# Seven block products in place of eight in the second feed-forward product of an attention and feed-forward kernel

## The chip, the cores and the metric

The kernel runs on one core of a Trainium2 chip, as one launch. The metric is the device time of that launch in microseconds; lower is better.

## The reference

Cosine attention over 8 batches of 12 heads, 448 positions of 64 values, and then a feed-forward block with a hard-swish over all 3584 tokens:

```python
q_n = q / (np.linalg.norm(q, axis=-1, keepdims=True) + 1e-06)
k_n = k / (np.linalg.norm(k, axis=-1, keepdims=True) + 1e-06)
scores = np.matmul(q_n, k_n.transpose(0, 1, 3, 2)) / tau
scores = scores - np.max(scores, axis=-1, keepdims=True)
attn = np.exp(scores)
attn = attn / (np.sum(attn, axis=-1, keepdims=True) + 1e-09)
x = np.matmul(attn, v)            # to (8 * 448, 12 * 64)
h = x @ w_in                      # 768 x 2048
relu6 = np.clip(h + 3.0, 0.0, 6.0)
g = h * relu6 / 6.0
return (g @ w_out)                # 2048 x 768, fp32
```

## The kernel before

**Tiling.** An *item* `i` is a pair of heads of one batch; a batch `b` has six, so there are 48 items. For an item, `scores` (L394) makes seven matmuls in four groups: the groups 0 to 2 have two matmuls each, with 64 rows of the array apiece, the fourth has one. `exps` (L412, ScalarE) turns them into `at`, `values` (L433) multiplies by `v` into the PSUM tile `PV`, `finish_values` (L453 and L454, VectorE) divides by the row sums, and a transposing DMA (`back_crossbar`, `back_two`) puts the result into `xT`, the input of the feed-forward block for this batch.

Around this, GpSimd squares the raw q and k (`square`, L203), normalises them (`normalise`, L246) and casts v (`vcast`, L265); VectorE sums the squares (`reduce`, L215); ScalarE makes the inverse norms (`norms`, L231 to L234). SP issues the loads (`load_qk`, `load_v`), the transposes and the stores. Raw items lie in 7 buffers, values in 3, squares in 2.

The feed-forward block is cut into *units*. `mm1_unit(b, fc)` is one of 16 slices of `x @ w_in` of a batch: six matmuls of 448 columns (L513) into one PSUM bank, then `relu` on ScalarE (L522) and `product` on VectorE (L528), which reads the bank too and writes the slice of g, in bf16, to `gT`. Only `product` frees the bank. `mm2_unit(b, t, m)` is one token tile of 128 and one half of 384 output columns of `g @ w_out`: 16 matmuls (L549), then a copy out of PSUM (L560 on ScalarE and L562 on VectorE by turns) and two stores.

**Order.** Every engine works through its own instructions in the order in which the program issues them; waits between engines are put in by data. The program's order is written by hand: up to item 17 in the strings of `PLAN`, from then on in a loop over items (L699 to L742). An iteration issues on TensorE: the score groups 0 to 2 of item `i`, the rest of the values of item `i - 1`, the fourth score group of `i`, then this iteration's units, and at last the first group of values of `i`.

**Banks.** After the start the PSUM has a ring of six banks, which `scores` and all units take by turns (`next_bank`). The groups 0 to 2 of an item take six, so each bank of the ring, the sixth being that of the unit issued just before.

**Where the units go.** `units[i]` holds the units of iteration `i`. Six iterations, `n` = 0 to 5, make a *turn*: in the turn of batch `b`, the `mm1_unit`s of batch `b - 1` and the `mm2_unit`s of `b - 2` are spread over them. Each list ends with the `mm2_unit`s:

```python
units[(b + 1) * HP + n] = carry + lag[: n_lag[n]] + u if n == 0 else carry + u + lag[: n_lag[n]]
```

(here `u` are `mm1_unit`s, and for n = 0 from the third batch on `u` is empty). What is left after item 47 runs in the tail: the rest of batch 6, then batch 7. The last unit of all is split into two halves of 192 columns.

`gT` has two tiles, each for two batches, 896 columns. An odd batch has four token tiles and an even one three, since the 64 tokens that an even batch leaves over are joined with 64 of the next.

Of the kernel before, what the change touches and what calls it, by code (L numbers as in the profile page):

```python
# [61 lines left out]
def kernel(  # L62
# [39 lines left out]
    gT = [const.tile([128, FCN, 2 * S], BF16, name=f"gT{i}", tag=f"gT{i}") for i in range(2)]  # L102
# [11 lines left out]
    NV, NR = 3, 7  # L114
    vr = [const.tile([128, 4, 5, D], FP32, name=f"vr{i}", tag=f"vr{i}") for i in range(NV)]
    NVX = 4
    vx = [const.tile([128, 8, D + 1], BF16, name=f"vx{i}", tag=f"vx{i}") for i in range(NVX)]
    raws = [const.tile([128, 2, 7, D], FP32, name=f"raw{i}", tag=f"raw{i}") for i in range(NR)]
    sqs = [const.tile([128, 2, 7, D], FP32, name=f"sq{i}", tag=f"sq{i}") for i in range(2)]
# [46 lines left out]
    def load_qk(j, *heads):  # L166
        needs(("NM", j - NR))
        raw_of[j] = raws[j % NR]
# [9 lines left out]
    def load_v(d):  # L178
        needs(("VC", 2 * (d - NV)), ("VC", 2 * (d - NV) + 1))
        b, n = 2 * d // HP, 2 * d % HP  # L180
        for g in range(2):
            f = v[b, HP * g + n : HP * g + n + 2].rearrange("i (p c) d -> p i (c d)", c=7)
            t = vr[d % NV][:, 2 * g : 2 * g + 2, :, :].rearrange("p i c d -> p i (c d)")
            for half in range(2):
                o = t[64 * half : 64 * half + 64, :, (1 - half) * D : (5 - half) * D]
                nc.sync.dma_start(out=o, in_=f[:, :, 3 * half * D : (3 * half + 4) * D])

    def square(j, e, c0, n):

        heads = range(c0 // 7, (c0 + n - 1) // 7 + 1) if j < 2 else (0, 1)  # L190
        needs(("RE", j - 2), *(("LQ", j, g) for g in heads))
        if j not in sq_of:
            sq_of[j] = sqs[j % 2], []
# [63 lines left out]
    def vcast(i, e):  # L257
        needs(("LV", i // 2), ("VA", i - NVX, 3))
        t = vr[i // 2 % NV][:, i % 2, 1:5, :]
# [247 lines left out]
    def mm1_unit(b, fc):  # L507
        needs(*(("CX", i) for i in range(b * HP, (b + 1) * HP)))
        assert len(weights) <= 6 - 2 * (2 * fc // FCN)
        x, g, c0 = xT[b % 2], gT[(b // 2) % 2], (b % 2) * S  # L510
# [29 lines left out]
    def mm2_unit(b, t, m, end=None):  # L540
        assert not weights
        g = gT[(b // 2) % 2]
        ps, key = bank_of(None, 1)
        width = MH if end is None else MH // 2
        cols = slice(m * MH + width * (end or 0), m * MH + width * (end or 0) + width)
        for fc in range(FCN):
            c0 = (S + SR) * (b % 2) + 128 * t if t < 3 else SM
            lhs = g[:, fc, c0 : c0 + 128]
            nc.tensor.matmul(  # L549
                ps[:, 0:width],  # L550
                lhs,
# [3 lines left out]
            )  # L555

        def store():
            o = sb.tile([128, MH], FP32, name="o", tag="o", bufs=4)
            if on_act:
                nc.scalar.copy(out=o[:, 0:width], in_=ps[:, 0:width])  # L560
            else:
                nc.vector.tensor_copy(out=o[:, 0:width], in_=ps[:, 0:width])  # L562
            unread[key] = 0
            for e in range(2):
                if t < 3:
                    r = out[b * S : (b + 1) * S].rearrange("(p c) m -> c p m", c=7)[2 * t + e + b % 2]
                else:
                    r = out[(b - 1 + e) * S : (b + e) * S].rearrange("(p c) m -> c p m", c=7)[6 * (1 - e)]
                eng = nc.scalar if end == 1 and e else nc.sync
                eng.dma_start(out=r[:, cols], in_=o[64 * e : 64 * e + 64, 0:width])  # L570

        evac_n[0] += 1
        on_act = evac_n[0] % 2 == 1
        post["a" if on_act else "v"].append(store)

    def second(b):
        nt = 3 + b % 2
        u = [(mm2_unit, b, t, m) for t in range(nt) for m in range(2)]
        return u if b < B - 1 else u[:-1] + [u[-1] + (0,), u[-1] + (1,)]

    units = {}
    carry, lag = [], []
    for b in range(B - 1):
        first = [(mm1_unit, b, fc) for fc in range(FCN)]
        n_lag = [0, 0, 1, 1, 2, 2] if b == 1 else [1, 1, 1, 1, len(lag) // 2 - 2, len(lag) // 2 - 2]
        n_first = [1, 3, 3, 3, 2, 2] if carry else [3, 3, 2, 2, 2, 2]
        if b > 1:
            n_first = [0, 3, 3, 3, 3, 2]  # L590
# [194 lines left out]
```

## Time and profile before

| | us |
|---|---|
| median of 3 runs | 423.14 |
| lowest, highest | 422.41, 423.39 |
| profiled execution: its span, from the first to the last instruction | 420.0 |

The profiled execution stands for itself: its span leaves out what lies before the first and after the last instruction, and is 3.1 us under the median of the runs. The granted clock was 0.999.

Some groups of the page that the change touches:

| line, engine | what | count | mean ns of one |
|---|---|---|---|
| L513 TensorE | `mm1_unit`, 448 columns, into M, Y and Z | 768 | 353 |
| L549 TensorE | `mm2_unit`, 384 columns | 880 | 326 |
| L549 TensorE | `mm2_unit`, 192 columns | 32 | 246 |
| L522 ScalarE | relu out of PSUM | 128 | 650 |
| L528 VectorE | product out of PSUM to bf16 | 128 | 620 |
| L560 ScalarE | copy of 384 out of PSUM | 28 | 478 |
| L562 VectorE | copy of 384 out of PSUM | 27 | 558 |
| L203 GpSimd | squares of 896 | 36 | 1679 |
| L246 GpSimd | normalise 896 | 44 | 1686 |
| L265 GpSimd | cast of 512 | 44 | 631 |

How to read it: a matmul's time runs from its issue to its modelled end; the next is issued long before that, so the time that TensorE needs for one is the distance between starts (0.19 us for 448 columns). In the timeline a row is one or several instructions on an engine: start, length, engine, line, operation, tiles, shape, count, and in square brackets how long the engine had been idle and what ended that. In the table by stretches each engine has its busy time and, in brackets, its instructions.

### The profile page before, as it was taken

Reading aid. Unit: us, or ns where it says so; the run is one execution under the profiler, and the core shown is the slowest. Engines: PE = TensorE matmul, PEld = TensorE weight load, DVE = VectorE, ACT = ScalarE, POOL = GpSimd, SP = SyncE. Lnnn points to the kernel's source line nnn. Section 1 sums busy time; section 2 is a strip of 40 time slices with the busy share of each in tenths; the row PEclk is TensorE's granted clock in tenths of the full one; section 3 lists DMA queues with packets and bytes.
Section 4 is the critical chain, followed back from the end, with each engine's and each line's share of the span. In section 5 each row is a group of like instructions: output and inputs, shape, how many; then the busy total and the mean of one; then the engine's idle time right before and its main releaser. Section 6 shows DMA issues by size and latency. Waiting matters only on the chain.

```text
span 420.0 us, 9243 instructions
## 1 busy us (share of the span) xinstructions
PE 412.6 (98%) x3600; PEld 244.6 (58%) x3600; DVE 217.3 (52%) x419; ACT 271.0 (65%) x591; POOL 183.6 (44%) x190
## 2 busy tenths in 40 slices
PE   7999999999999999999999999999999999999996
PEld 5666556556665565555565555555555555655554
DVE  6898677855345654455536454465454443315410
ACT  6899988887558666757747765866765774105400
POOL 7899646444237347257356355365462200000000
PEclk9999999999999999999999999999999999999999
DMA  8999999789796965966885858756953441330033
GB/s 296 311 235 248 182 270 229 154 152 242 202 181 133 190 162 132 179 166 140 190 196 118 191 146 171 186 157 135 193 158 72 85 66 34 70 75 21 0 77 75
DMA packets 91563, 65.29 MB, mean 155 GB/s; under 512 B 56064, under 2 KB 89984, under 8 KB 91520
## 3 DMA queue, kind: packets, MB, share of 16 engines
q1 hardware_dynamic: 87728, 58.37, 59.8%
q0 software_dynamic: 3712, 6.29, 8.6%
q8 instruction: 28, 0.46, 0.5%
q14 instruction: 15, 0.12, 0.1%
q10 hardware_dynamic: 80, 0.05, 0.0%
HBM read 47.19 MB, written 11.01 MB: 139 GB/s over the span
## 4 chain that ended last, share of the span: by engine, by line
PE 96%; DVE 1%; POOL 1%; DMA 1%; ACT 0%; issue 0%; ACTq 0%; DVEq 0%
PE M L513 24%; PE M L549 23%; PE PV L433 12%; PE Z L549 7%; PE M L394 6%; PE Y L513 6%; PE Y L549 6%; PE Z L513 5%; PE Y L394 2%; PE Z L394 1%; PE PV L620 1%; PE SC L394 1%; POOL nrm L246 1%; DMA raw<-in_k_dram 1%; PE Z L291 1%; DVE n L215 0%
## 5 line engine op out<-in xcount | busy, mean ns | idle before, releaser
L549 PEld LDWEIGHTS <-gT 128*128 128x128 bf16 x912 | 88.6, 98 | 58.4
L412 ACT ACTIVATE at<-M 128x448 bf16<-128x448 f32 x199 | 96.8, 567 | 31.2 <-PE M L394 18.9
L513 PEld LDWEIGHTS <-w_in_sb 128*128 128x128 bf16 x768 | 73.7, 98 | 65.8 <-issue 2.7
L513 PE MATMUL M<-xT,w_in_sb 128*128 128x448 bf16 x522 | 107.3, 353 | 0.0
L549 PE MATMUL M<-w_out_sb,gT 128*128 128x384 bf16 (+1 forms) x592 | 99.3, 324 | 0.0
L246 POOL TENSOR_TENSOR nrm<-raw,r 128x896 bf16<-128x896 f32 (+1 forms) x48 | 77.7, 1624 | 43.8 <-ACT r L234 34.7
L528 DVE SCALAR_TENSOR_TENSOR gT<-u,M 128x448 bf16<-128x448 bf16 x87 | 54.0, 620 | 52.3 <-ACT u L522 50.8
L203 POOL TENSOR_TENSOR sq<-raw 128x896 f32<-128x896 f32 (+3 forms) x39 | 63.4, 1627 | 9.9 <-DMA raw<-in_k_dram 4.8
L433 PEld LDWEIGHTS <-at 128*128 128x128 bf16 x1344 | 53.5, 98 | 24.4 <-issue 16.8
L522 ACT ACTIVATE u<-M,bias 128x448 bf16<-128x448 f32 x87 | 56.5, 650 | 16.6 <-PE M L513 15.4
L433 PE MATMUL PV<-vx,at 128*128 128x65 bf16 (+1 forms) x1344 | 64.0, 198 | 0.3 <-DVE on L454 0.2
L215 DVE TENSOR_REDUCE n<-sq 128x14 f32<-128x896 f32 (+1 forms) x50 | 51.8, 1041 | 3.8 <-ACT sq L201 3.6
L351 POOL COPY km<-tT 64x128 bf16<-64x128 bf16 x34 | 9.8, 289 | 96.8 <-DMA tT<-nrm 46.4
L412 ACT ACTIVATE at<-Z 128x448 bf16<-128x448 f32 x48 | 27.1, 565 | 12.5 <-PE M L394 12.4
L560 ACT COPY o<-M 128x384 f32<-128x384 f32 (+1 forms) x19 | 8.9, 470 | 40.5 <-PE M L549 40.4
L562 DVE COPY o<-M 128x384 f32<-128x384 f32 x18 | 10.0, 558 | 47.0 <-PE M L549 32.6
L454 DVE TENSOR_TENSOR on<-PV,rc 128x512 bf16<-128x512 f32 x48 | 33.2, 691 | 1.7
L394 PE MATMUL M<-tT,kz 64*128 64x448 bf16 (+1 forms) x175 | 32.6, 353 | 0.0
L549 PE MATMUL Z<-w_out_sb,gT 128*128 128x384 bf16 (+1 forms) x176 | 29.1, 319 | 0.0
L265 POOL CAST vx<-vr 128x512 bf16<-128x512 f32 x44 | 27.6, 631 | 1.5 <-DMA vr<-in_v_dram 1.5
L453 DVE RECIPROCAL rc<-PV 128x8 f32<-128x8 f32 x48 | 9.9, 207 | 34.9 <-PE PV L433 34.2
L412 ACT ACTIVATE at<-Y 128x448 bf16<-128x448 f32 x47 | 26.7, 569 | 1.7 <-PE Z L394 1.5
(78 smaller groups left out, 352.6 us busy)
## 6 DMA issues: line engine op xcount, KB each, us to landing
vr<-in_v_dram SPq DMA_DIRECT2D x96, 128.0 KB, 4.2
raw<-in_k_dram SPq DMA_DIRECT2D x24, 448.0 KB, 4.4
raw<-in_q_dram SPq DMA_DIRECT2D x24, 448.0 KB, 4.3
out_dram<-o SPq DMA_DIRECT2D x110, 96.0 KB, 2.2
w_in_sb<-in_moe_w_in_dram POOLq DMA_DIRECT2D x4, 768.0 KB, 12.2
w_out_sb<-in_moe_w_out_dram POOLq DMA_DIRECT2D x4, 768.0 KB, 9.2
tT<-nrm SPq DMA_TRANSPOSE x34, 3.3
xT<-on SPq DMA_TRANSPOSE x25, 3.9
```

Source lines behind the costliest of these rows:

```text
L203: engines[e].tensor_tensor(out=o, in0=i, in1=i, op=ALU.mult)
L215: nc.vector.tensor_reduce(out=n2s[d % 2][:, j % 2, c], in_=sq[:, :, :, :].rearrange("p g c d -> p (g c) d")[:, c, :], axis=AX.X, op=ALU.add,)
L246: engines[e].tensor_tensor(out=nrm[:, :, g, :].rearrange("p c g d -> p g c d"), in0=raw_of[j][:, g, :, :], in1=rs[d % 2][3][:, j % 2, :] . ...
L265: (engines[e].copy if e == "a" else engines[e].tensor_copy)(out=o, in_=f)
L394: nc.tensor.matmul(o, ks, qt[rows], start=True, stop=True)
L412: nc.scalar.activation(out=o, in_=x, func=AF.Exp, scale=inv_tau)
L433: nc.tensor.matmul(o, at[:, n, q_cols(i // HP, j)], mv, start=(name == "A0" and j % 2 == 0), stop=last, skip_group_check=True,)
L454: nc.vector.tensor_tensor(out=on[:, :, :, :].rearrange("p (b j) h d -> p b (j h) d", b=2), in0=pv4[:, :, :, 0:D], in1=rc[:, :, :].to_broad ...
L513: nc.tensor.matmul(ps[:, 0:S], w_in_sb[:, cc, fc * 128 : (fc + 1) * 128], x[:, cc, 0:S], start=(cc == 0), stop=(cc == CC - 1),)
L522: nc.scalar.activation(out=u[:, :], in_=ps[:, 0:S], func=AF.Relu, bias=half_bias, scale=1.0 / 6.0)
L528: nc.vector.scalar_tensor_tensor(out=g[:, fc, c0 : c0 + S], in0=u[:, :], scalar=1.0, in1=ps[:, 0:S], op0=ALU.min, op1=ALU.mult,)
L549: nc.tensor.matmul(ps[:, 0:width], lhs, w_out_sb[:, fc, cols], start=(fc == 0), stop=(fc == FCN - 1),)
```

## The change

**The products.** Two token tiles and the two halves of the output columns, with g and `w_out` split into even and odd slices `fc`, are four block products of two terms each: eight products of eight matmuls. From batch 2 on these are replaced by Strassen's seven: with A for g and B for `w_out`, sums of blocks of A and of B are formed first, seven products "1" to "7" of eight matmuls are made, and their sums are the four results. `product_unit` makes one of them. "2" is added in PSUM on top of "4" in the same bank, "5" on top of "3" and "6" on top of "1", after the first of each has been read: "4" is copied by ScalarE to `d`, "3" is added to it by VectorE, "2" and "5" are copied out and stored, GpSimd makes two differences from them, and VectorE adds those to "1", "6" and "7". An odd batch is two pairs of tiles. An even batch is one pair and a single tile, which `single_unit` makes in the old number of products but in four units of 192 columns.

**The sums.** `weight_sums` makes the sums of `w_out`, on VectorE, in the turn of batch 3: three into the new tile `w_sum`, and two (`y3`, `y4`) in place in `w_out_sb`, each once the old units of batch 1 have read that half. `g_sums` makes those of g, on VectorE, in bf16, twice for each batch, after the slices fc = 7 and fc = 15: five operations, some in place, and a sixth for the single tile. `g_left` copies the 64 columns that an even batch leaves over.

**The layout.** `gT` is one tile for even and one for odd batches. `w_sum` takes the place of two raw buffers, one value buffer and one square buffer, which are used until it is written; from then on there are 5, 2 and 1.

**The order.** The units of an iteration are put together by `turn`. The iterations up to item 17 and their `PLAN` are as they were.

```diff
+    def raw_before(j):
+        return j - 7 if j < 26 else j - 5
...
+    def value_buffer(d):
+        return vr[d % 3 if d < 12 else 1 + d % 2]
+    def square_buffer(j):
+        return sqs[j % 2 if j < 20 else 0]
...
-        x, g, c0 = xT[b % 2], gT[(b // 2) % 2], (b % 2) * S
+        x, g, c0 = xT[b % 2], gT[b % 2], (b % 2) * SR
...
+    def weight_sums(what, c0, n):
+        w = w_out_sb[:, :, :].rearrange("p (c k) m -> p c k m", k=2)[:, c0 : c0 + n]
+        b11, b12, b21, b22 = (w[:, :, k, m] for k in range(2) for m in (LEFT, RIGHT))
...
+        o, x, y, op = {
+            "x1": (w_sum[:, 0, c0 : c0 + n, :], b11, b22, ALU.add),
+            "x2": (w_sum[:, 1, c0 : c0 + n, :], b11, b12, ALU.add),
+            "x3": (w_sum[:, 2, c0 : c0 + n, :], b21, b22, ALU.add),
+            "y3": (b12, b12, b22, ALU.subtract),
+            "y4": (b21, b21, b11, ALU.subtract),
+        }[what]
+        nc.vector.tensor_tensor(out=o, in0=x, in1=y, op=op)
...
+    def g_sums(b, half):
+        c = slice(half * KC // 2, (half + 1) * KC // 2)
+        n = 1 + b % 2
...
+        todo = [
+            (s6, a21, a11, ALU.subtract),
+            (a21, a21, a22, ALU.add),
+            (s7, a12, a22, ALU.subtract),
+            (a12, a12, a11, ALU.add),
+            (s1, a11, a22, ALU.add),
+        ]
+        if n == 1:
+            e = gT[0][:, :, 256:384].rearrange("p (c k) n -> p c k n", k=2)[:, c]
+            todo.append((gs[0][:, 3, c, :], e[:, :, 0, :], e[:, :, 1, :], ALU.add))
+        for o, x, y, op in todo:
+            nc.vector.tensor_tensor(out=o, in0=x, in1=y, op=op)
...
+    def product_unit(b, g, name, end=None):
...
+        base = {"2": "4", "5": "3", "6": "1"}.get(name)
+        if base is None:
+            banks[n + (name,)] = bank_of(None, 1)
+        ps, key = banks.pop(n + (base,)) if base else banks[n + (name,)]
+        c0, width = (0, MH) if end is None else (MH // 2 * end, MH // 2)
+        for c in range(KC):
+            nc.tensor.matmul(
+                ps[:, 0:width],
+                quarter(b, g, name, c),
+                w_quarter(name, c)[:, c0 : c0 + width],
+                start=(base is None and c == 0),
+                stop=(c == KC - 1),
...
+        def copied(t, cols, x):
+            o = out_tile()
+            nc.scalar.copy(out=o[:, :], in_=m)
+            parts[n, x] = o
+            done(t, o, cols)
+        def added(t, cols, x, c0=0):
+            o = out_tile()
+            nc.vector.tensor_tensor(out=o[:, 0:width], in0=m, in1=x[:, c0 : c0 + width], op=ALU.add)
+            done(t, o, slice(cols.start + c0, cols.start + c0 + width))
+        def finish():
+            if name == "4":
+                nc.scalar.copy(out=part("d"), in_=m)
+            elif name == "3":
+                d = parts[n, "d"][:, :]
+                nc.vector.tensor_tensor(out=d, in0=m, in1=d, op=ALU.add)
+            elif name == "2":
+                copied(t2, LEFT, "C21")
+            elif name == "5":
+                copied(t1, RIGHT, "C12")
+                d = parts[n, "d"][:, :]
+                nc.gpsimd.tensor_tensor(out=part("f"), in0=d, in1=parts[n, "C12"][:, :], op=ALU.subtract)
+                nc.gpsimd.tensor_tensor(out=d, in0=d, in1=parts[n, "C21"][:, :], op=ALU.subtract)
+            elif name == "1":
+                f = parts[n, "f"][:, :]
+                nc.vector.tensor_tensor(out=f, in0=m, in1=f, op=ALU.add)
+            elif name == "6":
+                added(t2, RIGHT, parts[n, "d"])
+            else:
+                added(t1, LEFT, parts[n, "f"], c0)
...
+    def firsts(b, *fcs):
+        u = []
+        for fc in fcs:
+            u.append((mm1_unit, b, fc))
+            if b > 1 and fc % KC == KC - 1:
+                u.append((g_sums, b, fc // KC))
+        return u
...
+    def turn(b, n):
+        fc = 3 * (n - 1)
+        f = firsts(b - 1, *range(fc, fc + 3 + (n == 5))) if n else []
+        if b % 2 == 0:
+            p = [
+                products(b - 2, 0, "4325"),
+                products(b - 2, 0, "16"),
+                products(b - 2, 0, "7"),
+                singles(b - 2, (0, 0), (0, 1)),
+                singles(b - 2, (1, 0)),
+                singles(b - 2, (1, 1)),
+            ][n]
+        else:
+            p = [
+                products(b - 2, 0, "4325"),
+                products(b - 2, 0, "16"),
+                products(b - 2, 0, "7") + products(b - 2, 1, "42"),
+                products(b - 2, 1, "35"),
+                products(b - 2, 1, "16"),
+                products(b - 2, 1, "7"),
+            ][n]
+        if n == 0:
+            return p if b % 2 else [(g_left,)] + p
+        if len(p) < 3:
+            return p[:1] + f[:2] + p[1:] + f[2:]
+        return mixed([p[1], p[0], p[2]], f)
...
+    for n in range(HP):
+        fc = 3 * (n - 1)
+        if n == 0:
+            u = [(g_left,)] + firsts(1, FCN - 2, FCN - 1) + [late.pop(0) for _ in range(3)]
+        else:
+            f = firsts(2, *range(fc, fc + 3 + (n == 5)))
+            u = [late.pop(0)] + f
+        x = [(weight_sums, w, c, 2) for w in ("x1", "x2", "x3") for c in range(0, KC, 2)][3 * n : 3 * n + 3]
+        if n == 4:
+            x = [(weight_sums, "y4", c, 2) for c in range(0, KC, 2)]
+        if n == 5:
+            x = [(weight_sums, "y3", c, 2) for c in range(0, KC, 2)]
+        units[3 * HP + n] = u[:1] + x + u[1:] if n else u[:-1] + x + u[-1:]
...
+    last += products(b, 0, "4325176") + products(b, 1, "43251")
+    last += [(product_unit, b, 1, "7", 0)] + products(b, 1, "6") + [(product_unit, b, 1, "7", 1)]
```

`mixed` takes units from its two lists by turns. In the loop, sums and `g_left` are issued just before the unit that follows them in the list; they are not counted as units.

## The prediction

> **What bounds the kernel now.** I read first the page's busy time and the chain that ended last:
>
> ```profile
> PE 412.6 (98%) x3600; PEld 244.6 (58%) x3600; DVE 217.3 (52%) x419; ACT 271.0 (65%) x591; POOL 183.6 (44%) x190
> ...
> PE 96%; DVE 1%; POOL 1%; DMA 1%; ACT 0%; issue 0%; ACTq 0%; DVEq 0%
> PE M L513 24%; PE M L549 23%; PE PV L433 12%; PE Z L549 7%; PE M L394 6%; PE Y L513 6%; PE Y L549 6%; PE Z L513 5%; PE Y L394 2%; PE Z L394 1%; PE PV L620 1%; PE SC L394 1%; POOL nrm L246 1%; DMA raw<-in_k_dram 1%; PE Z L291 1%; DVE n L215 0%
> ```
>
> TensorE is the chain, so a matmul taken away is time gained, unless something new stops TensorE. The table by stretches says that it has no slack, and that VectorE, where the change puts its additions, is half idle:
>
> ```profile
> 200.00:250.00 50.00, 50.00 (x430) 29.25 (x429) 25.79 (x45) 33.95 (x77) 25.41 (x25) 1.00 0.71 166
> ```
>
> (columns: PE, PEld, DVE, ACT, POOL.) The chain in order of time gives the prices on TensorE: a unit of `mm1_unit` 1.14 us, 16 matmuls of 384 columns 2.60 us, so 0.1625 us each. The last unit's halves of 192 columns took 1.32 and 1.33 us for 16:
>
> ```profile
> 286.62 1.14 PE M L513 x6
> 287.76 1.13 PE Y L513 x6
> 288.89 1.14 PE Z L513 x6
> 290.02 2.60 PE M L549 x16
> 292.63 0.24 PE PV L433 x8
> ```
>
> Then I looked at the place where one attention item hands over to the next, because the change alters what stands in front of it. The timeline of TensorE, and VectorE beside it:
>
> ```profile
> 252.21 0.41 PE L433 MATMUL PV<-vx,at 128*128 128x65 bf16 x8
> 252.55 0.55 PE L394 MATMUL M<-tT,kz 64*128 64x448 bf16 x3
> 252.75 0.35 PE L394 MATMUL Y<-tT,kz 64*128 64x448 bf16 x1
> 252.94 0.35 PE L394 MATMUL Z<-tT,kz 64*128 64x448 bf16 x1
> 253.03 0.35 PE L394 MATMUL M<-tT,kz 64*128 64x448 bf16 x1
> 253.31 0.89 PE L433 MATMUL PV<-vx,at 128*128 128x65 bf16 x20
> ```
> ```profile
> 252.41 0.56 DVE L562 COPY o<-M 128x384 f32<-128x384 f32 x1 [1.31 <-PE M L549]
> ```
>
> The six score matmuls take all six banks of the ring, so the sixth needs the bank of the unit issued last. Here that is an `mm2_unit`; VectorE had copied it out at 252.97, and the sixth score matmul began 0.06 us later, 0.09 after its partner. Where ScalarE makes the copy (268.77 plus 0.48) it comes in time. So the kernel as it is loses about 0.05 us at each hand-over, and the reader sees how tight the place is.
>
> **The change, part by part.**
>
> *Matmuls.* Batches 2 to 7 have nine pairs of token tiles (one in each even batch, two in each odd one). A pair took 64 matmuls and takes 56: 9 x 8 x 0.1625 = 11.7 us less. The single tile of batches 2, 4 and 6 keeps its work but in four units of 192 columns: 4 x 1.325 against 2 x 2.60, 0.1 us more each, 0.3. **Gain 11.4 us**.
>
> *The order at the hand-over.* Before, a stretch of units ended with `lag`, an `mm2_unit`. In `turn` it ends with `f[2:]` (or the last of `mixed`), an `mm1_unit`, whose bank is free only after ScalarE's relu and then VectorE's product. What that takes is in the rows of the last 16 `mm1_unit`s, where both engines are idle: TensorE went on to the next unit at 395.14, and
>
> ```profile
> 395.34 0.63 ACT L522 ACTIVATE u<-M,bias 128x448 bf16<-128x448 f32 x1 [0.50 <-PE M L513]
> ```
> ```profile
> 396.00 0.62 DVE L528 SCALAR_TENSOR_TENSOR gT<-u,M 128x448 bf16<-128x448 bf16 x1 [0.52 <-ACT u L522]
> ```
>
> so the bank is free 1.48 us after TensorE is. The sixth score matmul could begin 252.94 - 252.21 = 0.73 us after it, and with the 0.06 begins at 1.54: a stop of 0.81, against 0.05 now, 0.76 more. Everything behind it on TensorE waits: the values of the item before, its fourth score group, all units. The places: turn 3 ends five stretches so (n = 1 to 5), turns 4, 5, 6 five each, turn 7 four (no scores follow item 47): 24 x 0.76 = **18.2 us**. This alone is more than the gain.
>
> *The sums of g.* Additions of bf16 in SBUF are not in the trace. Bounds: the fp32 addition-like row at L203 on VectorE (896 elements, 1.081 us) is one element a cycle of 0.96 GHz plus 0.148; the bf16 copies (448 in 0.381, 384 in 0.344) are two a cycle plus the same. So 512 elements cost 0.415 to 0.68 us, 1024 0.68 to 1.22. I take the lower ends, the copies being the nearest in type; two of L341 take 0.61 us together, so successive operations overlap 0.075. Six of 512 (an even batch) then block VectorE 2.1 us, five of 1024 (odd) 3.1. VectorE's load rises by 10.4 us of these, 0.7 of `g_left` and 4.2 of adds out of PSUM in two turns (96.6 us, from one hand-over at 261.7 to the same one at 358.2), from 52 to about 68%: there is room on the average. But VectorE works in order. In n = 3 the sums of the first half stand between the products of f7 and f8, and f8's bank is the one that the scores need. From the moment TensorE leaves f7: turns 5 and 7: f7's product done 1.49, sums 3.6, f8's product 4.2; the sixth score matmul could start at 1.30 + 1.14 + 0.73 = 3.17, so the stop is 1.1, 0.3 beyond the 0.81. Turns 4 and 6: a half store to 1.85, sums 4.95, product 5.57, against 3.19: 2.45, 1.6 beyond. Turn 3: 4.2 against 1.87: 2.4, 1.55 beyond. Together 0.6 + 3.2 + 1.55 = 5.4 us. GpSimd collides with them: the one cast that met a VectorE operation with two SBUF inputs took 1.468 us against 0.612, and the VectorE operation 1.36 against 1.08, each waiting for the other. Five such blocks, each losing between nothing and a normalisation plus a cast (1.69 + 0.61 = 2.3 us); I take 0.65, some half of one GpSimd operation: 3.2. **8.6 us**.
>
> That bf16 additions run at two a cycle is also what the Trainium skill says ("VectorE: DVE Perf Modes", the perf-mode tier table: 1224 ns for 2048 elements); worked out from its 158 fixed cycles, an estimate, 512 elements would be 0.43 us, and the blocks 0.1 us longer. Against the change speaks its "SBUF — State Buffer", Who interferes with whom: an operation with two SBUF inputs contends with any GpSimd instruction that reads SBUF, bf16 or not. No row here shows a bf16 addition in such a meeting; were its rule without exception, the loss per block would lie nearer to 2.3 than to nothing, some 5 us more in all.
>
> *Weight sums.* 20 operations of 768 elements in turn 3, 0.55 us each by the same row. Those of x1 to x3 and y4 run while the unit of batch 1 in front of them (2.60 us) keeps TensorE; that is their cover, and without it they would cost up to 1.65. y3 must wait until that unit has read `w_out_sb`, then takes 2.0 us ahead of the products of f12 to f15; f15's just comes in time if GpSimd stays away, 1.9 late if it doesn't. **1.0 us**.
>
> *Chained products.* "2" waits for ScalarE's copy of "4", "5" for VectorE's add of "3", "6" for that of "1", which waits for GpSimd's subtraction (384 fp32: 0.83 us). "3" stands between the first two, 1.3 us, and hides a copy (0.48). At the start of turns 5 and 7 VectorE has f15's product (1.49), the sums (to 4.55), a reduce (5.55), `finish_values` (6.5), and only then "3" (7.1); "5" would start at 2.75 + 3 x 1.3 = 6.65: 0.45 each, 0.9. Turns 4 and 6: 6.1, nothing. In the tail's first boundary no scores stand in between: "3" done at 5.8, "5" wanted at 4.86, then the transpose of item 47 (3.9 us to landing) just comes in time: 1.05. The last pairs: 0.25 for "5", 0.2 for "6". **2.4 us**; bounds 1.5 and 4.
>
> *Buffers.* Fewer raw, value and square buffers make `load_qk`, `load_v` and `square` wait for something later. In the timeline the cast of an odd item's values ended at 260.7 and SP, with the stores ahead of it, issued that load at 264.3; squares start up to 2.8 us later (the reduce ended at 263.4, not 260.7), with nothing due for them until 267.4. What is queued behind the load on SP is transposes due an item later. Nothing, covered by that slack of 3.5 us; if it is eaten, SP's transposes come late by what is missing. SP also issues four more half stores per single, 0.57 us each, in a queue that has a third of its time free.
>
> *Sum.* -11.4 + 18.2 + 8.6 + 1.0 + 2.4 = +18.8 on the profiled 420.0, so 438.8; the median of the runs is 3.1 above that span, and 423.1 + 18.8 = **442 us**. Its own range: stops of 0.70 net, no collisions, 24 x 0.70 + 5.4 + 1.5 = 23.7, 435, and some 4 for what I may have overlooked: 431; above, every collision at 2.3, y3 at 1.9, chains at 4: 41.5, 453.
>
> **The rivals.** (a) *The matmuls decide and the rest is hidden*: 423.1 - 11.4 = 411.7, to 419 with the smaller losses. For it: TensorE is 96% of the chain, VectorE half idle. Against it: the 0.09 above, which shows that the sixth bank is waited for. It decides if a hand-over loses less than 11.4/24 = 0.47 us with nothing else. (b) *A wash*: stops of half the size and few collisions; 423 +- 3. (c) *VectorE decides*: additions at one element a cycle. The blocks become 3.7 and 5.8 us, so n = 3 costs 18.8 with collisions, the chained products 14.3, y3 2.9: 423.1 - 11.4 + 18.2 + 18.8 + 14.3 + 2.9 = 466. For it: fp32 rows at one a cycle; against it the bf16 copies.
>
> **How the numbers follow.** Forecast 0.66, (a) 0.17, (b) 0.07, (c) 0.10. Within 0.2% is what a measurement here can't tell from no change. Faster: (a) and 0.03 of (b), 0.20; same 0.02; slower 0.78. The range holds the forecast's bulk (0.63), (b) and half of (a): 414 to 458; the forecast's own is 431 to 453.
>
> **What would show it.** TensorE's matmuls at 3600 - 72 + 96 - 8 = 3616, the added ones being half width; a gap of 0.8 us before the sixth score matmul of an item, ended by L528's successor; the largest gaps in n = 3; bf16 additions of 0.42 and 0.68 us, some longer where GpSimd is busy. If the sixth score matmul follows its partner within 0.2 us, my main term is wrong and (a) is right.

## The result, and the profile after

| | us |
|---|---|
| before, median | 423.0 |
| after, median of 4 runs (lowest, highest) | 457.39 (456.05, 458.27) |
| ratio after to before, 95% interval | 1.081 (1.079 to 1.083) |
| profiled execution after: span (before: 420.0) | 456.3 |

The changed kernel is slower by 34 us; the forecast was 19 us slower. In the experiments below the kernel before was timed again each time (medians of 422.6 to 422.8 us), and each ratio is against that. The page's busy times and chain after:

```profile
PE 419.6 (92%) x3616; PEld 249.2 (55%) x3616; DVE 284.5 (62%) x537; ACT 275.5 (60%) x596; POOL 204.9 (45%) x208
...
PE 74%; DVE 15%; ACT 5%; issue 2%; DMA 1%; POOL 1%; SPq 0%; ACTq 0%; DVEq 0%
```

TensorE has 3616 matmuls, as foreseen. It is *busier* than before (419.6 against 412.6 us) although it has 11.4 us less to do: part of the time its matmuls run slower, and the first part of each stop counts as busy, because the matmul before it is still running. And it holds only 74% of the chain, VectorE 15%. The list of waits (engine, line, releaser: total us, times, longest) says where VectorE comes in:

```profile
PE Y L424 <- DVE gT L558: 17.6, 7, 4.6
```

L424 is `scores` in the changed file, L558 `product`, which frees the bank of an `mm1_unit`. An ordinary hand-over, in the timeline of TensorE:

```profile
134.63 0.41 PE L463 MATMUL PV<-vx,at 128*128 128x65 bf16 x8
134.96 0.55 PE L424 MATMUL M<-tT,kz 64*128 64x448 bf16 x3
135.17 0.35 PE L424 MATMUL Y<-tT,kz 64*128 64x448 bf16 x1
135.46 0.35 PE L424 MATMUL Z<-tT,kz 64*128 64x448 bf16 x1
136.17 0.35 PE L424 MATMUL M<-tT,kz 64*128 64x448 bf16 x1 [0.36 <-DVE gT L558]
```

The sixth score matmul begins 136.17 - 134.63 = 1.54 us after TensorE has left the unit, where an unhindered one begins at 0.73: a stop of 0.81, the number of the prediction. Nineteen of the 24 hand-overs look so: 15.4 us. The other five are those with n = 3, where the sums of g stand in VectorE's queue. The one of turn 5, on TensorE, VectorE and GpSimd:

```profile
264.33 0.41 PE L463 MATMUL PV<-vx,at 128*128 128x65 bf16 x8
...
269.98 0.53 PE L424 MATMUL Y<-tT,kz 64*128 64x448 bf16 x1 [4.57 <-DVE gT L558]
270.44 1.50 PE L463 MATMUL PV<-vx,at 128*128 128x65 bf16 x20
```
```profile
263.79 0.42 DVE L663 TENSOR_TENSOR gs<-gT 128x512 bf16<-128x512 bf16 x1
264.24 1.10 DVE L663 TENSOR_TENSOR gT<-gT 128x512 bf16<-128x512 bf16 x1
265.27 1.21 DVE L663 TENSOR_TENSOR gs<-gT 128x512 bf16<-128x512 bf16 x1
266.51 1.79 DVE L663 TENSOR_TENSOR gT<-gT 128x512 bf16<-128x512 bf16 x1
268.23 1.16 DVE L663 TENSOR_TENSOR gs<-gT 128x512 bf16<-128x512 bf16 x2
269.31 0.61 DVE L558 SCALAR_TENSOR_TENSOR gT<-u,Y 128x448 bf16<-128x448 bf16 x1
```
```profile
263.95 1.11 POOL L735 TENSOR_TENSOR f<-d,o 128x384 f32<-128x384 f32 x1 [2.99 <-ACT o L715]
265.15 1.05 POOL L736 TENSOR_TENSOR d<-d,o 128x384 f32<-128x384 f32 x1
266.16 1.86 POOL L276 TENSOR_TENSOR nrm<-raw,r 128x896 bf16<-128x896 f32 x1
267.98 0.80 POOL L295 CAST vx<-vr 128x512 bf16<-128x512 f32 x1
```

The first sum runs alone and takes the 0.42 us that were foreseen. From then on a sum and a GpSimd operation go by turns: each sum lasts about as long as the GpSimd operation beside it (1.10 beside 1.11, 1.21 beside 1.05, 1.79 beside 1.86). Six sums that need 2.1 us alone take 5.6 (263.79 to 269.39). The start to start time is 269.98 - 264.33 = 5.65, so the stop is 5.65 - 0.73 = 4.92. Over turns 3 to 7 the stops of n = 3, read so, are 3.72, 3.39, 4.92, 3.39 and 3.06: 18.5 us, where the prediction has 5 x 0.81 + 8.6 = 12.7. (Some expectations below have the first three 0.18 us longer: they count the slow score matmul behind the stop as well.) The stops of all 24 hand-overs are 33.9 us; the list of waits has 25.5 for them, and the 8.4 between is what TensorE counts as busy.

Look also at the values' matmuls behind that stop: 20 of them took 1.50 us, and 0.90 elsewhere. The table by stretches around it, in stretches of 3.41 us (columns: length, PE, PEld, DVE, ACT, POOL, granted clock, DMA share, GB/s):

```profile
262.12:265.53 3.41, 3.29 (x27) 1.70 (x26) 2.96 (x7) 2.49 (x7) 1.50 (x2) 1.00 0.13 27
265.53:268.94 3.41, 0.00 (x0) 0.00 (x0) 3.38 (x3) 1.82 (x5) 3.25 (x3) 1.00 0.59 165
268.94:272.35 3.41, 2.38 (x23) 1.60 (x23) 2.32 (x6) 0.55 (x2) 1.35 (x1) 0.50 0.44 117
272.35:275.76 3.41, 3.41 (x11) 1.52 (x10) 1.11 (x2) 0.54 (x1) 2.53 (x3) 0.50 0.61 129
275.76:279.17 3.41, 3.41 (x21) 1.87 (x20) 1.37 (x3) 1.27 (x2) 0.00 (x0) 1.00 0.23 52
```

After the stop TensorE's clock is granted at half, exactly 0.50, for two such stretches, while it has work. This happens behind each of the five long stops and nowhere else in the middle of the run. The items behind them are 9.7 us longer than the same work at full clock, and the tails of the stops themselves 0.5 us: 10.2 us that no step of the prediction has.

Where the 36.3 us between the spans (456.3 against 420.0) went:

| | foreseen | found |
|---|---|---|
| matmuls taken away | -11.4 | -11.4 (not measured apart) |
| 24 hand-overs, those of n = 3 included, beyond the 0.05 each of before | +26.8 | 15.4 + 18.5 - 1.2 = +32.7 |
| halved clock behind the long stops | none | +10.2 |
| chained products: starts of turns 4 to 7, tail | +2.4 | 2 x 0.67 + 2 x 0.46 + 1.4 = +3.6 |
| weight sums `y3` | +1.0 | 0 |
| start, and end after the last matmul (5.11 against 3.83) | none | 0.4 + 1.3 = +1.7 |
| sum | +18.8 | +36.8 |

The right column is 0.5 us more than the difference of the spans; I can't place that.

### The profile page after: what moved, and what is told of

Its sections match the earlier page's. It is cut to its first block, busy times and chain, and to the rows that moved or that the text cites. A ratio compares the mean times of both kernels' runs of the same rounds, so it can differ in the third digit from the quotient of the medians.

```text
span 456.3 us, 9498 instructions
## 1 busy us (share of the span) xinstructions
PE 419.6 (92%) x3616; PEld 249.2 (55%) x3616; DVE 284.5 (62%) x537; ACT 275.5 (60%) x596; POOL 204.9 (45%) x208
## 4 chain that ended last, share of the span: by engine, by line
PE 74%; DVE 15%; ACT 5%; issue 2%; DMA 1%; POOL 1%; SPq 0%; ACTq 0%; DVEq 0%
PE M L543 22%; PE M L694 11%; PE PV L463 9%; PE M L593 6%; DVE gs L663 4%; PE Y L543 4%; ACT u L552 4%; DVE gT L558 4%; PE Z L543 4%; PE M L424 3%; DVE gT L663 3%; PE M L757 2%; PE Z L593 2%; PE Z L424 2%; PE PV L880 1%
## 5 line engine op out<-in xcount | busy, mean ns | idle before, releaser
L543 PE MATMUL M<-xT,w_in_sb 128*128 128x448 bf16 x552 | 115.3, 357 | 0.0
L558 DVE SCALAR_TENSOR_TENSOR gT<-u,M 128x448 bf16<-128x448 bf16 x92 | 57.0, 620 | 59.3 <-ACT u L552 58.7
L276 POOL TENSOR_TENSOR nrm<-raw,r 128x896 bf16<-128x896 f32 (+1 forms) x42 | 68.4, 1633 | 32.2 <-ACT r L264 24.6
L233 POOL TENSOR_TENSOR sq<-raw 128x896 f32<-128x896 f32 (+2 forms) x32 | 52.7, 1647 | 45.2 <-DVE n L245 37.5
L735 POOL TENSOR_TENSOR f<-d,o 128x384 f32<-128x384 f32 x9 | 9.1, 1015 | 80.8 <-ACT o L715 80.8
L245 DVE TENSOR_REDUCE n<-sq 128x14 f32<-128x896 f32 (+1 forms) x39 | 41.0, 1055 | 2.1 <-ACT sq L231 1.0
L694 PEld LDWEIGHTS <-gT 128*128 128x128 bf16 x288 | 28.1, 98 | 21.4 <-issue 3.5
L424 PE MATMUL M<-tT,kz 64*128 64x448 bf16 (+1 forms) x175 | 34.1, 353 | 4.6 <-DVE gT L558 4.6
L694 PE MATMUL M<-w_sum,gs 128*128 128x384 bf16 (+1 forms) x184 | 35.3, 340 | 0.0
L424 PE MATMUL Y<-tT,kz 64*128 64x448 bf16 (+1 forms) x42 | 15.4, 366 | 17.6 <-DVE gT L558 17.6
L694 PEld LDWEIGHTS <-gs 128*128 128x128 bf16 x224 | 22.5, 101 | 15.7 <-issue 2.9
L694 PE MATMUL M<-w_out_sb,gT 128*128 128x384 bf16 x160 | 28.8, 326 | 1.6 <-DVE d L729 1.6
L593 PEld LDWEIGHTS <-gT 128*128 128x128 bf16 x224 | 22.0, 99 | 14.4 <-issue 0.7
```

The costliest lines, as they stand in the source:

```text
L233: engines[e].tensor_tensor(out=o, in0=i, in1=i, op=ALU.mult)
L245: nc.vector.tensor_reduce(out=n2s[d % 2][:, j % 2, c], in_=sq[:, :, :, :].rearrange("p g c d -> p (g c) d")[:, c, :], axis=AX.X, op=ALU.add,)
L276: engines[e].tensor_tensor(out=nrm[:, :, g, :].rearrange("p c g d -> p g c d"), in0=raw_of[j][:, g, :, :], in1=rs[d % 2][3][:, j % 2, :] . ...
L424: nc.tensor.matmul(o, ks, qt[rows], start=True, stop=True)
L543: nc.tensor.matmul(ps[:, 0:S], w_in_sb[:, cc, fc * 128 : (fc + 1) * 128], x[:, cc, 0:S], start=(cc == 0), stop=(cc == CC - 1),)
L558: nc.vector.scalar_tensor_tensor(out=g[:, fc, c0 : c0 + S], in0=u[:, :], scalar=1.0, in1=ps[:, 0:S], op0=ALU.min, op1=ALU.mult,)
```

## The experiments

Two theories stood at the beginning. *Order*: the time goes because of what stands last before a hand-over, an `mm1_unit`, and because sums of g stand before its product; Strassen's products by themselves bring what their matmuls say. The rival: *VectorE* (or GpSimd) has too much to do now, whatever the order, and the stops would move elsewhere.

**1. The product unit last, sums where they were.**

```diff
-        if len(p) < 3:
-            return p[:1] + f[:2] + p[1:] + f[2:]
-        return mixed([p[1], p[0], p[2]], f)
+        if len(p) == 3:
+            return mixed(f, [p[1], p[0], p[2]])
+        if len(p) == 2:
+            return p[:1] + f + p[1:]
+        if n == 5:
+            return f[:-1] + p + f[-1:]
+        return f + p
...
+        if n and n < 5:
+            u = u[1:] + u[:1]
         units[3 * HP + n] = u[:1] + x + u[1:] if n else u[:-1] + x + u[-1:]
```

> The changed kernel with another order of units only: in 18 of the 24 stretches a unit of the second product (or a half store) stands last, not a unit of the first; the sums of g stay behind the eighth unit of the first product. Theory A (the sixth score matmul waits for the bank of the unit issued last): the stops of 0.81 us at those hand-overs fall to 0.1 or less, 14 of them outside n = 3 and so some 11 us; the stops in n = 3 change little, by the additions that no longer meet the GpSimd differences. 440 to 447 us. Theory B (VectorE and GpSimd are simply given too much work): the same work is done, so within 1% of 457. Theory C (the halved clock is the main loss): the stops in n = 3 stay near 3 us, the halved stretches with them, so the gain is no more than that of A.

Measured: 445.07 us, ratio 1.052 (1.047 to 1.056). The new order reaches 23 of the 24 stretches, not the 18 of the expectation. Of the 19 ordinary stops, 18 fall from 0.81 to between 0 and 0.35; the one behind n = 5 of turn 3, where an `mm1_unit` is still last, stays at 0.81. That is 11.8 us less. The long stops of n = 3 stay (2.0 to 3.9 us), with a halved clock behind each (mean clock 0.963, lower than the changed kernel's 0.97): so the 12 us that came back are hand-overs.

**2. The sums of g behind the last unit, order of units as changed.**

```diff
         f = firsts(b - 1, *range(fc, fc + 3 + (n == 5))) if n else []
+        if n == 3:
+            f = [x for x in f if x[0] is not g_sums] + [x for x in f if x[0] is g_sums]
```

The same two lines stand in the loop of turn 3.

> The changed kernel with one thing moved: in n = 3 the sums of g of the first half are issued behind the last unit of the stretch in place of ahead of it. Theory A: the five stops in n = 3 (3.90, 3.57, 5.10, 3.39 and 3.06 us, 19.0 together) become 0.81 as everywhere else, 15 us less. Theory C (a stop of some 3 us halves the clock for a while after it): the five stretches of halved clock, some 10 us of delay, go too, so 431 to 437 us in all and a granted clock of 0.99 throughout. If the clock has another cause, it stays near 0.97 and the time at 441 or more. Theory B: within 1% of 457.

Measured: 438.77 us, ratio 1.039 (1.037 to 1.040), 1.8 us above the expectation. All five long stops are gone, the other stops are 0.81 as in the changed kernel, and the clock is 0.991. Two new places are behind the miss. In turn 5 the add of "1" now stands behind the sums, and "6" waits for it (1.7 us). And the four `y4` subtractions now meet GpSimd. In the timelines of VectorE and GpSimd:

```profile
157.59 4.72 DVE L640 TENSOR_TENSOR w_out_sb<-w_out_sb 128x768 bf16<-128x768 bf16 x4
162.24 1.67 DVE L558 SCALAR_TENSOR_TENSOR gT<-u,M 128x448 bf16<-128x448 bf16 x3
```
```profile
158.55 2.00 POOL L276 TENSOR_TENSOR nrm<-raw,r 128x896 bf16<-128x896 f32 x1
160.50 0.94 POOL L295 CAST vx<-vr 128x512 bf16<-128x512 f32 x1
```

Four operations that need 4 x 0.55 = 2.2 us alone take 4.72, three products wait behind them, TensorE stops for 2.77 us and its clock is halved for 6.8 us.

**3. Both.** The product unit last, and the sums behind it, in all turns. The diff is against experiment 1; the loop of turn 3 gets the same.

```diff
+        s = [x for x in f if x[0] is g_sums]
+        f = [x for x in f if x[0] is not g_sums]
         if len(p) == 2:
-            return p[:1] + f + p[1:]
-        if n == 5:
-            return f[:-1] + p + f[-1:]
-        return f + p
+            return p[:1] + f + p[1:] + s
+        return f + p + s
```

> Both orders together: units of the second product last, sums of g behind them. Theory A with C: 457.4 less 18 stops of 0.76, less 15 and less 10, so 416 to 421 us, which is below the kernel before: the seven products pay once nothing stands in front of the bank that the scores need. Theory B: within 1% of 457.

Measured: 421.9 us (10 runs, 420.89 to 424.52), ratio 0.998 (0.995 to 1.000): level with the kernel before, and 0.9 above the expectation's range. The clock is 1.00. So the order, with the clock that hangs on it, is worth 35.5 us (457.39 - 421.9). VectorE has the same 537 instructions as after, and they hold up little: the rival falls. What is left is many small waits: 1.88 us at `y4`, 0.81 behind the one `mm1_unit` that is still last, four of some 0.5 at the starts of turns, ten of 0.2 to 0.35 because the bank of a pair's first product is now among the first that the scores want, 1.19 for the add of "1", and the start and the end.

**4. The order alone, without Strassen.** The kernel before, its one line turned so that `mm1_unit`s stand last:

```diff
-            units[(b + 1) * HP + n] = carry + lag[: n_lag[n]] + u if n == 0 else carry + u + lag[: n_lag[n]]
+            units[(b + 1) * HP + n] = carry + lag[: n_lag[n]] + u
```

> The kernel before, with nothing of the seven products: only the order in a stretch is turned round, units of the second product first and units of the first product last, as in the changed kernel. Theory A (the bank of the last unit): every hand-over behind such a stretch stops TensorE 0.81 us in place of 0.04 on the average; there are 24 or 25 of them, so 441 us (18 more), with the clock at 1.00 since no stop is long. Theory B (the work of the additions): no additions here, so no change, within 0.5% of 423.

Measured: 442.62 us, ratio 1.047 (1.043 to 1.050); +19.9 us. In its trace 22 of the 24 hand-overs stop for 0.81 us and two for 1.24, which less the 0.05 each of before makes 19.1. No product, no sum and no buffer of the change is in this kernel. In its waits for that line:

```profile
PE M L394 <- DVE gT L528: 6.7, 16, 0.6
PE Z L394 <- DVE gT L528: 2.3, 5, 0.6
PE Y L394 <- DVE gT L528: 1.3, 3, 0.5
```

16 + 5 + 3 = 24 waits, one for each place that the prediction counts, none over 0.6 us; its clock was 0.996, from one halving at 12.5 us, long before these places. (A wait is shorter than the stop, since the matmul before still runs when the stop begins.)

**5. GpSimd's work out of the way of the sums.** The changed kernel, in n = 3 with the norms, the normalising and the cast issued right behind the squares:

```diff
         prepare(("SQ", i + 5, "p", 0, 7))
+        if i % HP == 3:
+            prepare(("NO", (i + 3) // 2), ("NM", i + 3, "p"), ("VC", i + 2, "p"))
...
-        if not even:
+        if not even and i % HP != 3:
             prepare(("NO", (i + 3) // 2))
...
-        prepare(("NM", i + 3, "p"), ("VC", i + 2, "p"), ("RE", i + 5))
+        if i % HP != 3:
+            prepare(("NM", i + 3, "p"), ("VC", i + 2, "p"))
+        prepare(("RE", i + 5))
```

> The changed kernel; in the iterations n = 3 the inverse norms, the normalisation and the cast of GpSimd are issued right behind the squares, so that GpSimd is done with them before the sums of g begin; the same work. If GpSimd's meetings with the sums set the length of the stops in n = 3, those of turns 3, 4 and 6 (3.90, 3.57, 3.39 us) fall to 2.3 to 2.6, while turns 5 and 7, where the two GpSimd differences stay in the way, change by less than the length of a normalisation (1.7); the clock falls in fewer of them; 450 to 454 us. If the additions are slow by themselves, the stops stay within 0.3 us and the time at 457.

Measured: 449.63 us, ratio 1.064 (1.061 to 1.067): 7.8 us come back from GpSimd's timing alone, 0.4 more than the expectation's range. The stops of n = 3 are now 3.73, 2.54, 2.64, 2.53 and 2.65, 14.1 in all against 18.5. In turns 4 and 6 that is what the prediction has for sums without a collision (2.45). Two of the five went another way than expected: turn 5 fell by 2.3, more than the 1.7 allowed, and turn 3 didn't fall. In turn 5 two of six sums still meet the two differences:

```profile
261.35 0.42 DVE L663 TENSOR_TENSOR gs<-gT 128x512 bf16<-128x512 bf16 x1
261.80 0.42 DVE L663 TENSOR_TENSOR gT<-gT 128x512 bf16<-128x512 bf16 x1
262.14 1.22 DVE L663 TENSOR_TENSOR gs<-gT 128x512 bf16<-128x512 bf16 x1
263.40 1.10 DVE L663 TENSOR_TENSOR gT<-gT 128x512 bf16<-128x512 bf16 x1
264.42 0.75 DVE L663 TENSOR_TENSOR gs<-gT 128x512 bf16<-128x512 bf16 x2
```

which is 1.5 us more than 2 x 0.42, and explains 2.64 against the 1.1 foreseen. In turn 3 the sums run clean here and the stop stays, because the meeting has only moved. The normalisation and the cast now run beside the three weight sums ahead of the product, which take 2.72 us; in the changed kernel, where GpSimd rests at that time, they take 1.49. The rows of this run and, last, of the changed kernel:

```profile
149.13 2.72 DVE L640 TENSOR_TENSOR w_sum<-w_out_sb 128x768 bf16<-128x768 bf16 x3
148.39 1.69 POOL L276 TENSOR_TENSOR nrm<-raw,r 128x896 bf16<-128x896 f32 x1
150.03 0.94 POOL L295 CAST vx<-vr 128x512 bf16<-128x512 f32 x1
```
```profile
149.44 1.49 DVE L640 TENSOR_TENSOR w_sum<-w_out_sb 128x768 bf16<-128x768 bf16 x3
```

The rest of the gain, 7.8 - 4.4 = 3.4 us, fits the clock: half clock for four stretches of 3.41 us where there were seven.

**6. The clock, measured by itself.** The kernel before, with 7 to 15 useless writes of the output tile on VectorE ahead of the last copy of ten hand-overs (that copy is always VectorE's there), so that TensorE stops for a length that I choose:

```diff
+    hold = [0]
+    HOLD = {25: 8, 27: 10, 29: 9, 31: 13, 33: 11, 35: 9, 37: 15, 39: 10, 41: 7, 43: 12}
...
+            for _ in range(held):
+                nc.vector.memset(o[:, :], 0.0)
```

> The kernel before, with 7 to 15 writes of zeros by VectorE put into the output tile just ahead of the last copy out of PSUM in ten stretches, so that TensorE stops there for about 1.7 to 5.1 us; what is computed stays the same. It measures the clock by itself. Theory C: behind stops above some length near 3 us (the changed kernel's were 3.06 to 5.10) the granted clock falls to one half for a few us and the matmuls of 384 columns take up to 0.33 us; behind shorter ones it stays at 1.00. Rival: the clock is lowered by the number of stops, or by what VectorE does beside them, and not by the length of one: then it falls behind none of these or behind all.

One run, 484.53 us, clock 0.95. The stops came out at 1.5 to 7.1 us. The clock went to 0.50 behind eight of the ten, for 3.4, 6.8 or 10.2 us; a stop of 3.38 us had no halving behind it, one of 2.95 had. The length of the stop alone doesn't decide. What does is seen when the *places* are compared: in this trace the halvings begin at 205.82, 229.71, 250.19, 274.08, 315.04, 342.35, 362.83 and 383.31 us (from the clock in slices of 0.5 us), and the distances are 7.0, 6.0, 7.0, 12.0, 8.0, 6.0 and 6.0 times 3.413. In the trace of after they begin at 156.30, 210.92, 268.94, 326.97 and 381.58: 16.0, 17.0, 17.0 and 16.0 times 3.413. So time is cut into windows of 3.413 us that no stop sets going, and the clock changes only at their borders. The share of each window in which TensorE had matmuls running, in the six traces that had halvings in the middle (after, experiments 1, 2, 5, 6 and 7), from 120 us to the last matmuls, and the clock of the window behind it:

```
window at full clock, busy share     next window
0.00 to 0.46                         halved in all 22
0.49, 0.54, 0.55                     full
0.54, 0.55                           halved
0.61 and over                        full in all
window at half clock, busy share     next window
up to 0.89                           halved again in all
0.91, 0.92, 0.94                     full
0.95                                 halved again
1.00                                 full in all
```

A window that is busy for less than about half of its time is nearly always paid for with half the clock in the next one. One exception lies outside the table, at the end of experiment 3: the window from 414.02 us was busy for 1.49 us, 0.43 of it, and the next one was full. The clearest pair is in experiment 5: TensorE was idle for 2.19 us in turn 4 and for 2.19 us in turn 6.

```profile
208.71:212.12 3.41, 1.22 (x23) 0.78 (x22) 3.27 (x5) 2.66 (x6) 0.03 (x1) 1.00 0.71 192
212.12:215.53 3.41, 3.41 (x22) 2.80 (x19) 1.17 (x3) 0.54 (x1) 3.41 (x3) 0.50 0.74 165
314.52:317.93 3.41, 2.55 (x26) 1.42 (x24) 3.31 (x6) 1.74 (x4) 0.65 (x2) 1.00 0.20 32
317.93:321.34 3.41, 2.09 (x33) 1.72 (x33) 3.11 (x6) 2.17 (x5) 1.06 (x1) 1.00 0.85 235
321.34:324.75 3.41, 3.41 (x24) 2.00 (x22) 1.03 (x3) 1.08 (x2) 2.82 (x3) 1.00 0.80 181
```

In turn 4 the stop fell into one window (busy 1.22 of 3.41) and cost the next one half its clock. In turn 6 a border cut it in two (2.55 and 2.09 busy), and it cost nothing more.

**7. What was left in experiment 3.** A pair's first product comes later in an iteration, `y4` stands behind the last unit, at the start of a turn the reduce and the squares stand behind the second product, and the last stores of "6" and "7" are split over two queues. The diff, in parts, is against experiment 3.

```diff
-            return p[:1] + f + p[1:] + s
+            return f[:2] + p[:1] + f[2:] + p[1:] + s
...
+        if n == 4:
+            u, x = u + x, []
...
-            eng = nc.scalar if end == 1 and e else nc.sync
+            eng = nc.scalar if e and (end == 1 or late_store[0]) else nc.sync
...
+        if i % HP == 0 and i > FIRST:
+            do("UU", n - 1)
+            prepare(("RE", i + 4))
+            prepare(("SQ", i + 5, "p", 0, 7))
```

> The kernel with both orders, and the waits that are still in it taken on one by one: the first product of a pair later in its stretch so that its bank is not the first that the scores need, the subtraction of the weights behind the last unit in n = 4, the reduce and the squares at the start of a turn behind the second product, and the last stores on two queues. What that kernel still waits for beyond the one before: stops of 0.2 to 0.35 us at some ten hand-overs (2.5), 1.2 for one product, four times 0.5 at the start of a turn, 1.8 in turn 3, 1.3 at the end. Theory A: 413 to 417 us, 1.5 to 2.4% below the kernel before. If the seven products have another cost that is not a wait of TensorE, it stays at 420 or more.

Measured: 417.88 us (6 runs, 416.17 to 422.79; the ratio leaves out the one of 422.79), ratio 0.989 (0.985 to 0.992), 0.9 over the expectation's range; faster than both kernels. One long stop is left. On VectorE and GpSimd:

```profile
248.75 2.65 DVE L665 TENSOR_TENSOR gs<-gT 128x512 bf16<-128x512 bf16 x2
251.33 1.07 DVE L245 TENSOR_REDUCE n<-sq 128x14 f32<-128x896 f32 x1
...
254.22 0.55 DVE L742 TENSOR_TENSOR f<-M,f 128x384 f32<-128x384 f32 x1
```
```profile
248.51 1.86 POOL L276 TENSOR_TENSOR nrm<-raw,r 128x896 bf16<-128x896 f32 x1
250.32 0.80 POOL L295 CAST vx<-vr 128x512 bf16<-128x512 f32 x1
```

The add of "1" (L742) stands behind sums that again go by turns with GpSimd, and "6" waits for it: 2.35 us, and a window of half clock.

**8. Experiments 7 and 5 together.**

> The kernel of the run of 417.88 us with one more move: in the hand-overs that have sums of g (n=3), the norms, the normalising product and the cast of the values for GpSimd are issued right behind the squares, ahead of the other units, as in the run that moved them alone in the changed kernel. Theory: the 2.35 us stop that was left, and the halved clock behind it, come from sums of g and finish_values that collide with GpSimd's four operations; with GpSimd done earlier the sums run at .42 and .69 us each, the stop goes to under .8 us and the clock stays at 1.00: 417.9 - 1.6 (stop) - 1.5 (halved clock) = 414 to 416 us. Rival, that the stop comes from the sums' own length and their place ahead of the add of "1": the stop stays at 2 us or more and the time is 416.5 to 419 us.

Measured: 416.14 us (5 runs, 415.49 to 416.27), ratio 0.984 (0.982 to 0.986). On VectorE, the same sums:

```profile
247.46 0.42 DVE L665 TENSOR_TENSOR gs<-gT 128x512 bf16<-128x512 bf16 x1
247.91 0.42 DVE L665 TENSOR_TENSOR gT<-gT 128x512 bf16<-128x512 bf16 x1
248.25 0.42 DVE L665 TENSOR_TENSOR gs<-gT 128x512 bf16<-128x512 bf16 x1
248.71 0.42 DVE L665 TENSOR_TENSOR gT<-gT 128x512 bf16<-128x512 bf16 x1
249.05 1.56 DVE L665 TENSOR_TENSOR gs<-gT 128x512 bf16<-128x512 bf16 x2
```

Only one of six still meets a difference. The 2.35 us stop is gone; what stops are left in the loop are 0.85 us at a chained product, 0.81 at one hand-over, 1.39 in turn 3 and some of 0.15 to 0.36. The mean clock of the run is 1.000. The time is 0.1 above what the theory expected; the rival for it (the sums' own length) had the stop stay, which it did not. The intervals of experiments 7 and 8 overlap at 0.985 to 0.986, so the 1.7 us between them rest on the trace more than on the times.

## Why the prediction came out as it did

The direction and its reason were right; the size was 15 us too small (442 against 457.4), or 17.5 between the spans: the forecast put 3.1 us on top of its span, and the changed kernel's median is 1.1 above its own. Of the 17.5, 16 are one place, the sums of g in n = 3. The result lies above the forecast's own range (431 to 453); that it is still inside the wide one (414 to 458), by 0.6 us, is luck.

- **The hand-over.** "begins at 1.54: a stop of 0.81" is what the trace has, to the hundredth, in 19 places; experiment 4 gets 24 such stops with nothing else of the change, and experiment 1 takes 18 of the 19 away. Rival (a), that the rest is hidden, fell with it; the 0.09 us in the profile of before had said so.
- **The sums of g, alone.** bf16 additions of 0.42 and 0.68 us, as taken; rival (c) had 0.68 and 1.22, and a time of 466. That 457 lies nearer to it than to 442 is chance: its mechanism is not there. The sums without collisions were right too, 2.45 foreseen and 2.53 found in turns 4 and 6 of experiment 5. For turn 3 (2.4 foreseen) no run shows them so: in the changed kernel the sums met GpSimd there (3.72), in experiment 5 the weight sums did (3.73). Less the 1.23 us that the weight sums lost by it, the stop would be 2.5, an estimate.
- **The collisions**: the step that was mis-sized. "I take 0.65, some half of one GpSimd operation", from the one cast that met a VectorE operation. That row shows one meeting. But a block of six sums meets every GpSimd operation that is queued, one after another, because each side gets its turn when the other is done: in turn 5 four operations of 0.80 to 1.86 us, and the block is 3.5 us longer, above the upper bound of 2.3, since I had not put the two differences into that bound. I costed those two at 0.83 us each as work and forgot them as obstacles (they take 1.00). The prediction's upper sum, 41.5, is 41.0 by its own terms, which leaves its 453 as it is. Stops of n = 3: 18.5 us against 12.7.
- **The Trainium skill's rule** that the prediction put against its own figure ("SBUF — State Buffer", Who interferes with whom: an operation with two SBUF inputs contends with a GpSimd instruction that reads SBUF) holds here for bf16 additions: 0.42 us alone, 1.10 to 1.79 beside GpSimd. The prediction had said that such a reading would cost some 5 us more; the stops of n = 3 were 5.8 more.
- **The clock**: the step that is missing. The prediction took a stop for its own length. Behind each of the five long stops TensorE worked at half clock, 10.2 us in all; more than half of the difference between the spans. A granted clock of 0.999 in the profile of before showed no such case, since its list of waits has none over 0.2 us on TensorE in the middle of the run.
- **Chained products.** The starts of turns 5 and 7 cost 0.46 each, 0.45 foreseen; those of turns 4 and 6, where nothing was foreseen, 0.67 each. The tail cost 1.4, foreseen 1.05 + 0.45 = 1.5.
- **What cost nothing.** Fewer buffers, as foreseen (the list of waits has none of TensorE on a load); `y3`, where 1.0 was taken (the stop behind it is 0.81 like the others).
- **The end.** 1.3 us, not foreseen: of the last six stores five stand one behind the other on SP.

Of the difference of 17.5 us between foreseen and found spans, the clock has 10.2, the hand-overs with sums and collisions 5.9, chained products 1.2, start and end 1.7, less 1.0 for `y3` and the 0.5 that I can't place.

## What to carry to other kernels

Before a burst that takes all buffers of a ring, put the unit whose buffer comes free soonest in front of it, and put work of the freeing engine behind that unit and not before it; here this order was worth more (35 us) than the 11.4 us of matmuls that the change saves. Where a stop of TensorE can fill more than half of a window of 3.4 us, add what the halved clock behind it costs (1.4 to 2.8 us a stop in the changed kernel). When a series of two-input operations is put on VectorE, add up every GpSimd operation that can fall beside it, not one.

## What the runs showed of the hardware

- TensorE's clock is granted at 1.00 or 0.50 by windows of 3.413 us, whose borders run on without regard to the program (they lie elsewhere in each run: 2.70, 1.02 and 0.50 us past a multiple of 3.413 in the traces of after and of experiments 6 and 5). The Trainium skill has the window, its free running and the two states ("TensorE: Matmul & The Clock Gate", Part 1: The HAM clock gate), and gives one idle window as the condition for the lower one. These runs agree on the window and not on the condition: in the table a window that was busy for up to 46% of its time was enough in 22 of 22, a stop of 2.03 us in experiment 1 did it with 55%, and one of 3.38 us across a border did not. The share is not the whole rule either: around 0.55 the clock went both ways, and once, at the end of experiment 3, a window of 43% had a full one behind it. What decides there stays open.
- To come back a half-clock window had to be busy for more than about 0.9 of its time; one that held the rest of a stop (0.70 busy) was followed by another half one, which is why some episodes last 6.8 us.
- Where VectorE's two-input additions in SBUF and GpSimd's operations were both queued, they went by turns, one for one, in each meeting shown above (in turn 5 of the changed kernel additions of 1.10, 1.21 and 1.79 us, 0.42 alone, beside operations of 1.11, 1.05 and 1.86).
- Left open: a kernel with a long stop spreads more from run to run (in experiment 7 416.17 us at a clock of 0.999 and 420.43 at 0.992; in experiment 8, without the stop, 415.5 to 416.3 at 0.998 to 1.000). That the window borders fall elsewhere each time would explain it, but the windows can be seen only in the one run of each that was traced.
